# The last half chunk of a projection done as 64-row matmul pairs that open their sums, four output tiles at a time

## The chip, the cores and the metric

One core of a Trainium2 chip runs the kernel. The metric is the device time of one execution in microseconds (us). Times of runs below are medians of six executions, those of the kernel before medians of eleven (six in the first comparison). The kernel before takes 150.12 us (three executions, 150.08 to 150.18). The profile's span is shorter than that by about 1.7 us, because it runs from the first to the last recorded instruction.

TensorE is called PE below, its weight loads PEld, VectorE DVE, ScalarE ACT, GpSimd POOL and SyncE SP, as in the profile.

## The reference

Input x has 2048 tokens of 448 features. Two branches are mixed by a gate computed from each token:

```python
def reference(A_x, A_wqkv, A_w_phi, A_wo, B_x, B_w1, B_b1, B_w2, B_b2, gate_w):
    g = sigmoid((A_x * gate_w).sum(-1, keepdims=True))
    # A: linear attention, 16 heads of 28; phi is a pair of softmaxes of q @ w_phi and k @ w_phi
    o = num / den                      # phi_q @ (phi_k^T v)  over  phi_q @ sum(phi_k)
    a = o.reshape(S, 448) @ A_wo
    # B: dense 448 -> 1792 -> 448 with a tanh gelu
    b = gelu(B_x @ B_w1 + B_b1) @ B_w2 + B_b2
    return g * a + (1 - g) * b
```

In the kernel B's input is x too. The last stage works on 16 output tiles of 128 tokens. A tile's PSUM sum `y` collects 14 matmuls of the dense product (1792 = 14 x 128) and the attention product, whose contraction is 448 = 3.5 x 128: three full chunks and half a chunk.

## The kernel before

The output stage of the kernel before, with cuts marked. `oT` holds the attention result transposed; `oT[:, 3]` has 64 rows of it, then a row of ones that multiplies b2 (stored as row 64 of `wo_sb[:, 3]`), then zeros.

```python
    def num_tile(t):                                    # numerators of tile t
        nm = ps2.tile([P, 512], F32, name="nm", tag="nm", bufs=2)       # two PSUM banks
        for x in range(NPR):                            # 8 matmuls of 58 columns
            nc.tensor.matmul(nm[...], lhsT=EqT[:, x, tok], rhs=KV[:, x, :], start=True, stop=True)
        ...                                             # VectorE: den, reciprocal, al
        nc.vector.tensor_tensor(out=o_tok[:, t % 4, 0:D]..., in0=nmv..., in1=al..., op=ALU.mult)
        nc.sync.dma_start_transpose(oT[:, :, tok], o_tok[:, t % 4, :])

    def dense_out(y, t, cols):
        for j in range(NJ):                             # 14 matmuls
            nc.tensor.matmul(y, lhsT=gel[...], rhs=w2_sb[:, j, cols], start=(j == 0), stop=False)

    def attn_out(y, t, cols):
        for c in range(NC4):                            # 4 matmuls, the last with 64 useful rows + b2
            nc.tensor.matmul(y, lhsT=oT[:, c, tok], rhs=wo_sb[:, c, cols],
                             start=False, stop=(c == NC4 - 1))
        res = work.tile([P, D], BF16, name="res", bufs=3)
        nc.scalar.activation(out=res[:, cols], in_=y, func=ACT.Copy, scale=ungate[:, t:t + 1])
        nc.sync.dma_start(out2[tok, cols], res[:, cols])
    ...
    for t in range(NT - 1):
        dense_out(y[:, 0:D], t, full)
        ...                          # numerators of t + 2 (up to 8), later of t + 3: one tile a turn
        while len(wait) > (1 if t < 4 else 0):
            attn_out(*wait.pop(0))
    ...                              # tile 15 in two column parts, 336 and 112
```

`y` has four PSUM banks, `nm` two. Earlier in the kernel the input projections already use 64-row pairs: two matmuls with 64 contraction rows each, one on the upper and one on the lower half of the array, run at the same time.

The softmax here doesn't subtract the row's maximum and nothing guards it: scores larger than these inputs give would overflow.

Of the kernel before, what the change touches and what calls it, by code (L numbers as in the profile page):

```python
# [7 lines left out]
ALU = mybir.AluOpType  # L8
ACT = mybir.ActivationFunctionType
# [4 lines left out]
D = 448  # L14
# [3 lines left out]
P = 128  # L18
NB = 4
NT = 16  # L20
NG = 4
GW = 112
NC4 = 4
NJ = 14
KW = 60
NPR = 8
PW = 56
NK = 7
HP = 64

BF16 = mybir.dt.bfloat16
F32 = mybir.dt.float32
# [3 lines left out]
def kernel(  # L36
# [14 lines left out]
    nc = tc.nc  # L51
# [4 lines left out]
    consts = ctx.enter_context(tc.tile_pool(name="consts", bufs=1))  # L56
    work = ctx.enter_context(tc.tile_pool(name="work", bufs=2))
# [6 lines left out]
    def wide(name):  # L64
        return ps.tile([P, 2, 512], F32, name=name, tag="acc", bufs=1)
# [11 lines left out]
    w2_sb = consts.tile([P, NJ, D], BF16, name="w2_sb")  # L77
    wo_sb = consts.tile([P, NC4, D], BF16, name="wo_sb")
    EqT = consts.tile([P, NPR, S], BF16, name="EqT")
    phq3 = consts.tile([P, 2, NPR, 2, HP], BF16, name="phq3")  # L80
    oT = consts.tile([P, NC4, S], BF16, name="oT")
    o_tok = consts.tile([P, 4, 512], BF16, name="o_tok")
    KV = consts.tile([P, NPR, PW + 2], BF16, name="KV")
    mask = consts.tile([P, PW + 2], BF16, name="mask")
# [5 lines left out]
    ungate = consts.tile([P, NT], F32, name="ungate")  # L90

    hold = ctx.enter_context(tc.tile_pool(name="hold", bufs=1))
    phik = hold.tile([P, NT, NPR, 2, HP], BF16, name="phik", tag="phik_gel")
    vaug = hold.tile([P, NT, NPR, PW + 2], BF16, name="vaug")

    atn = ExitStack()
    attn = atn.enter_context(tc.tile_pool(name="attn", bufs=1))
# [14 lines left out]
    def q_tok(u):  # L112
        if u == 7:
            return phq3[:]
        return phq[u // 4][:, u % 4].rearrange("p (i x s w) -> p i x s w", i=2, x=NPR, s=2)
# [31 lines left out]
    def swap_x(h, part=None):  # L147
# [4 lines left out]
        if part != "even":  # L152
# [29 lines left out]
                          in_=mask[:, PW:PW + 2, None].to_broadcast([P, 2, DH]))  # L182
# [56 lines left out]
    def k_both(base, xo, b1=False):  # L239
        pks = both("pk", Wpk, WkS, D, base, xo, b1)  # L240
        for m, pk in enumerate(pks):
            k_exp(base // 2 + m, pk)
        if b1:
            nc.scalar.copy(out=b1T[:], in_=pks[1][:, 1, 480:480 + NJ])
# [43 lines left out]
    def norm(dst, split):  # L288
        sums = work.tile([P, 32, 2], F32, name="sums", bufs=3)
        ph = dst.rearrange("p t x s w -> p (t x s) w")[:, :, 0:PW]  # L290
        ph = ph.rearrange("p y (h d) -> p y h d", d=DH)
        nc.vector.reduce_sum(out=sums[:], in_=ph, axis=AX.X)  # L292
        rec = work.tile([P, 32, 2], F32, name="rec", bufs=3)
        nc.vector.reciprocal(out=rec[:], in_=sums[:])  # L294
        parts = [(nc.vector, 0, split), (nc.gpsimd, split, 32)] if split else [(nc.gpsimd, 0, 32)]
        for eng, lo, hi in parts:
            eng.tensor_tensor(out=ph[:, lo:hi], in0=ph[:, lo:hi],  # L297
                              in1=rec[:, lo:hi, :, None].to_broadcast([P, hi - lo, 2, DH]),
                              op=ALU.mult)
# [4 lines left out]
    def q_norm(u):  # L304
        norm(q_tok(u), 0)
        for i in range(2):
            t = 8 * (u // 4) + 4 * i + u % 4
            nc.sync.dma_start_transpose(EqT[:, :, t * P:(t + 1) * P],
                                        q_tok(u)[:, i].rearrange("p x s w -> p (x s w)"))
# [45 lines left out]
    def kv_sum(acc, u):  # L355
        for t in (2 * u, 2 * u + 1):
            for x in range(NPR):
                nc.tensor.matmul(acc[:, 0, x * (PW + 2):(x + 1) * (PW + 2)],  # L358
                                 lhsT=phik[:, t, x, :, :].rearrange("p s w -> p (s w)"),
                                 rhs=vaug[:, t, x, :], start=(t == 0 and x == 0),  # L360
                                 stop=(t == NT - 1), skip_group_check=True)

    def kv_out(acc):
        nc.vector.tensor_tensor(
            out=KV[:], in0=acc[:, 0, 0:NPR * (PW + 2)].rearrange("p (x w) -> p x w", x=NPR),
            in1=mask[:, None, :].to_broadcast([P, NPR, PW + 2]), op=ALU.mult)
# [61 lines left out]
    nc.sync.dma_start(wo_sb[:, 0:3, :], A_wo[0:384, :].rearrange("(c p) n -> p c n", p=P))  # L428
    nc.sync.dma_start(wo_sb[0:64, 3, :], A_wo[384:448, :])
    nc.sync.dma_start(wo_sb[64:65, 3, :], B_b2[None, :])  # L430

    k_both(0, x0o)
    k_norm(0)
# [29 lines left out]
    def m_unit(h, j):  # L463
        hp = wide("hp") if h == 0 and j == 2 else pair("hp")
        for k in range(NK):
            for i in range(2):
                nc.tensor.matmul(hp[:, i, :],  # L467
                                 lhsT=w1_sb[i * HP:(i + 1) * HP, k, j * P:(j + 1) * P],
                                 rhs=x_half(i, k, h), start=(k == 0), stop=(k == NK - 1))
        if gel[h] is None:  # L470
            gel[h] = hold.tile([P, NJ, S // 2], BF16, name="gel1", tag="phik_gel")
        nc.scalar.activation(out=gel[h][:, j, :],  # L472
                             in_=hp[:].rearrange("p a b -> p (a b)"),
                             func=ACT.Gelu_apprx_tanh, bias=b1T[:, j:j + 1])

    def num_tile(t):
        tok = slice(t * P, (t + 1) * P)
        nm = ps2.tile([P, 512], F32, name="nm", tag="nm", bufs=2)
        for x in range(NPR):
            nc.tensor.matmul(nm[:, x * (PW + 2):(x + 1) * (PW + 2)], lhsT=EqT[:, x, tok],  # L480
                             rhs=KV[:, x, :], start=True, stop=True)
        nmv = nm[:, 0:NPR * (PW + 2)].rearrange("p (x w) -> p x w", x=NPR)
        den = work.tile([P, NPR, 2], F32, name="den", bufs=3)
        nc.vector.tensor_scalar(out=den[:], in0=nmv[:, :, PW:PW + 2], scalar1=1e-6, scalar2=None,  # L484
                                op0=ALU.add)
        nc.vector.reciprocal(out=den[:], in_=den[:])
        al = work.tile([P, NPR, 2], F32, name="al", bufs=3)
        nc.vector.tensor_scalar(out=al[:], in0=den[:], scalar1=eL[:, t:t + 1], scalar2=None,
                                op0=ALU.mult)
        nc.vector.tensor_tensor(  # L490
            out=o_tok[:, t % 4, 0:D].rearrange("p (x h d) -> p x h d", x=NPR, h=2),
            in0=nmv[:, :, 0:PW].rearrange("p x (h d) -> p x h d", h=2),
            in1=al[:, :, :, None].to_broadcast([P, NPR, 2, DH]), op=ALU.mult)
        nc.sync.dma_start_transpose(oT[:, :, tok], o_tok[:, t % 4, :])

    for n in range(2 * NJ):
        m_unit(n // NJ, n % NJ)
        if n < 8:
            q_norm((0, 1, 2, 3, 4, 5, 6, 7)[n])
        if n == 8:  # L500
            nc.sync.dma_start(w2_sb[:], B_w2.rearrange("(j p) n -> p j n", p=P))
        if n == 4:
            acc = wide("acc")
            for u in range(8):
                kv_sum(acc, u)
            kv_out(acc)
            gates()

    psx.close()
    ps2 = ctx.enter_context(tc.tile_pool(name="ps2", bufs=2, space=PSUM, reuse_waits="tile"))  # L510


    def dense_out(y, t, cols):
        for j in range(NJ):
            nc.tensor.matmul(y, lhsT=gel[t // 8][:, j, (t % 8) * P:(t % 8 + 1) * P],  # L515
                             rhs=w2_sb[:, j, cols], start=(j == 0), stop=False)

    def attn_out(y, t, cols):
        tok = slice(t * P, (t + 1) * P)
        for c in range(NC4):  # L520
            nc.tensor.matmul(y, lhsT=oT[:, c, tok], rhs=wo_sb[:, c, cols],  # L521
                             start=False, stop=(c == NC4 - 1))
        res = work.tile([P, D], BF16, name="res", bufs=3)
        nc.scalar.activation(out=res[:, cols], in_=y, func=ACT.Copy, scale=ungate[:, t:t + 1])  # L524
        nc.sync.dma_start(out2[tok, cols], res[:, cols])

    def y_tile():
        return ps2.tile([P, 512], F32, name="y", tag="y", bufs=4)

    y = y_tile()  # L530
    num_tile(0)
    num_tile(1)
    wait = []
    full = slice(0, D)
    for t in range(NT - 1):
        y = y_tile() if t else y
        dense_out(y[:, 0:D], t, full)
        wait.append((y[:, 0:D], t, full))
        for n in ([t + 2] if t < 6 else [8, 9] if t == 6 else [t + 3]):
            if n < NT:  # L540
                num_tile(n)
        while len(wait) > (1 if t < 4 else 0):
            attn_out(*wait.pop(0))
    for cols in (slice(0, 336), slice(336, D)):
        y = y_tile()[:, 0:cols.stop - cols.start]
        dense_out(y, NT - 1, cols)
        attn_out(y, NT - 1, cols)
# [1 line left out]
_INS = ['A_x', 'A_wqkv', 'A_w_phi', 'A_wo', 'B_x', 'B_w1', 'B_b1', 'B_w2', 'B_b2', 'gate_w']  # L549
_OUTS = [((1, 2048, 448), 'bfloat16')]  # L550
# [25 lines left out]
```

## Time and profile before

| what | value | where from |
|---|---|---|
| time | 150.12 us | median of 3 |
| span of the profile | 148.4 us | page |
| PE busy | 144.2 us, 97% | page, part 1 |
| output stage | 58.12 us | trace: start of the first numerator matmul (86.95) to start of the last matmul (145.08) |
| tail | 3.31 us | trace: start of the last matmul to the end of the span |

Starts are what to read on PE: a matmul's record is longer than the time for which it keeps the next one waiting (0.35 against 0.189 us at 448 columns). "Output stage" in this document always means the stretch defined in the table.

Two of the costliest groups of the page (line, engine, operation, shapes and count, then busy us and mean ns, then idle time before them), and the line of the DMA issues for the transposes (count, median us to landing):

```profile
L524 ACT ACTIVATE res<-y,ungate 128x448 bf16<-128x448 f32 (+2 forms) x17 | 10.4, 613 | 47.1 <-PE y L521 41.1
...
L521 PE MATMUL y<-wo_sb,oT 128*128 128x448 bf16 (+2 forms) x68 | 14.7, 341 | 0.0
...
oT<-o_tok SPq DMA_TRANSPOSE x16, 2.4
```

ScalarE evicts the output and waits for PE; PE waits for nobody (0.0 idle). A transpose takes 2.4 us from issue to landing in the median (tile 9's took 4.0).

### The profile page before, as it was taken

The page shows a single profiled execution, that of the slowest core. Times are in us where ns is not written, and L with a number is a line of the kernel's source. Part 1 is how long each engine was busy: PE and PEld are TensorE (multiplying, and loading weights), DVE is VectorE, ACT ScalarE, POOL GpSimd, SP SyncE. Part 2 cuts the span into 40 slices and gives each one's busy share as a digit, 9 for nine tenths or more (in the row PEclk, how much of TensorE's full clock was granted, in tenths as well). Part 3 has the DMA queues.
Part 4 walks back from the last instruction along what each step waited for, and adds up shares of the span by engine and source line. Part 5 has one row for each costly group of instructions (what it writes and reads, how often), then busy time and mean ns, then how long its engine had stood idle before and what let it go on. Part 6 is the DMA issues. An engine that isn't in the chain of part 4 may idle for free.

```text
span 148.4 us, 3123 instructions
## 1 busy us (share of the span) xinstructions
PE 144.2 (97%) x1302; PEld 75.7 (51%) x1302; DVE 79.5 (54%) x129; ACT 75.6 (51%) x93; POOL 68.4 (46%) x50
## 2 busy tenths in 40 slices
PE   7999999999999999999999999999999999999991
PEld 2674445554544944444444455555555555555561
DVE  3443799999999999999100046333336333333000
ACT  1656989988899337676777760111311111111121
POOL 7999999999877999929930000000000000000000
PEclk9999999999999999999999999999999999999999
DMA  4999999999400199990999903333212422223201
GB/s 144 239 234 208 171 180 214 218 217 214 107 2 2 24 175 142 191 180 15 169 174 200 313 0 71 62 75 70 67 65 70 102 67 70 71 71 76 79 31 31
DMA packets 44658, 17.85 MB, mean 120 GB/s; under 512 B 36706, under 2 KB 44644, under 8 KB 44644
## 3 DMA queue, kind: packets, MB, share of 16 engines
q1 hardware_dynamic: 43428, 16.99, 55.0%
q10 hardware_dynamic: 1152, 0.65, 1.6%
q8 instruction: 10, 0.16, 0.5%
q14 instruction: 4, 0.03, 0.1%
q0 software_dynamic: 64, 0.01, 0.0%
HBM read 6.11 MB, written 1.84 MB: 54 GB/s over the span
## 4 chain that ended last, share of the span: by engine, by line
PE 97%; ACT 0%; issue 0%; DVE 0%; ACTq 0%
PE hp L467 29%; PE y L515 29%; PE y L521 8%; PE pq L351 7%; PE v_ps L335 4%; PE pk L343 4%; PE pk L226 3%; PE acc L358 3%; PE nm L480 3%; PE warm_ps L389 2%; PE v_ps L212 2%; PE v_ps L226 2%; PE w_ps L253 1%; PE xp L372 1%; PE pk L229 1%; PE v_ps L229 0%
## 5 line engine op out<-in xcount | busy, mean ns | idle before, releaser
L515 PE MATMUL y<-w_sb,gel 128*128 128x448 bf16 (+2 forms) x238 | 45.2, 341 | 0.0
L467 PE MATMUL hp<-xT,w_sb 64*128 64x512 bf16 x196 | 42.6, 376 | 0.0
L467 PE MATMUL hp<-xS,w_sb 64*128 64x512 bf16 x196 | 42.6, 376 | 0.0
L472 ACT ACTIVATE gel<-hp,b1T 128x1024 bf16<-128x1024 f32 x28 | 30.8, 1111 | 13.2 <-PE hp L467 13.2
L524 ACT ACTIVATE res<-y,ungate 128x448 bf16<-128x448 f32 (+2 forms) x17 | 10.4, 613 | 47.1 <-PE y L521 41.1
L515 PEld LDWEIGHTS <-gel 128*128 128x128 bf16 x238 | 22.6, 98 | 19.6
L467 PEld LDWEIGHTS <-w_sb 64*128 64x128 bf16 x392 | 18.9, 94 | 23.1
L297 POOL TENSOR_TENSOR phik<-phik,rec 128x1792 bf16<-128x1792 bf16 (+1 forms) x8 | 24.9, 3127 | 1.7 <-DVE rec L294 1.6
L484 DVE TENSOR_SCALAR den<-nm 128x16 f32<-128x16 f32 x16 | 2.8, 174 | 42.7 <-PE nm L480 42.7
L292 DVE TENSOR_REDUCE sums<-phik 128x64 f32<-128x1792 bf16 x8 | 16.0, 1999 | 3.5 <-ACT phik L283 3.5
L521 PE MATMUL y<-wo_sb,oT 128*128 128x448 bf16 (+2 forms) x68 | 14.7, 341 | 0.0
L297 POOL TENSOR_TENSOR oT<-oT,rec 128x1792 bf16<-128x1792 bf16 x4 | 12.7, 3209 | 1.1 <-DVE rec L294 1.1
L351 PE MATMUL pq<-Wpq,xT 64*128 64x448 bf16 x56 | 11.4, 349 | 0.0
L351 PE MATMUL pq<-WqS,xS 64*128 64x448 bf16 x56 | 11.4, 349 | 0.0
L297 POOL TENSOR_TENSOR w_sb<-w_sb,rec 128x1792 bf16<-128x1792 bf16 x3 | 9.6, 3210 | 2.9 <-DVE rec L294 2.9
L490 DVE TENSOR_TENSOR o_tok<-nm,al 128x448 bf16<-128x448 f32 x16 | 10.0, 625 | 0.6
L294 DVE RECIPROCAL rec<-sums 128x64 f32<-128x64 f32 x16 | 8.9, 553 | 1.4
L200 DVE CAST vaug<-v_ps 128x896 bf16<-128x896 f32 x7 | 7.5, 1072 | 2.4 <-PE v_ps L212 2.1
L282 ACT ACTIVATE phik<-pk 128x896 bf16<-128x896 f32 x8 | 7.6, 953 | 1.5 <-PE pk L231 1.5
L292 DVE TENSOR_REDUCE sums<-oT 128x64 f32<-128x1792 bf16 x4 | 7.9, 1981 | 0.0
L283 ACT ACTIVATE phik<-pk 128x896 bf16<-128x896 f32 x8 | 7.7, 964 | 0.0
L521 PEld LDWEIGHTS <-oT 128*128 128x128 bf16 x68 | 5.6, 97 | 3.5
(111 smaller groups left out, 170.5 us busy)
## 6 DMA issues: line engine op xcount, KB each, us to landing
w_sb<-in_B_w_dram SPq DMA_DIRECT2D x4, 784.0 KB, 11.8
out_dram<-res SPq DMA_DIRECT2D x15, 112.0 KB, 1.9
w_sb<-in_B_w_dram SPq DMA_DIRECT2D x1, 1568.0 KB, 7.2
xS<-xT SPq DMA_DIRECT2D x2, 256.0 KB, 3.7
EqT<-in_A_x_dram ACTq DMA_DIRECT2D x1, 448.0 KB, 3.3
xS<-xT SPq DMA_DIRECT2D x2, 192.0 KB, 3.5
wo_sb<-in_A_wo_dram SPq DMA_DIRECT2D x1, 336.0 KB, 16.8
oT<-o_tok SPq DMA_TRANSPOSE x16, 2.4
```

Source lines behind the costliest of these rows:

```text
L282: nc.scalar.activation(out=dst[:, :, :, 0, 0:PW], in_=src, func=ACT.Exp)
L283: nc.scalar.activation(out=dst[:, :, :, 1, 0:PW], in_=src, func=ACT.Exp, scale=-1.0)
L292: nc.vector.reduce_sum(out=sums[:], in_=ph, axis=AX.X)
L294: nc.vector.reciprocal(out=rec[:], in_=sums[:])
L297: eng.tensor_tensor(out=ph[:, lo:hi], in0=ph[:, lo:hi], in1=rec[:, lo:hi, :, None].to_broadcast([P, hi - lo, 2, DH]), op=ALU.mult)
L351: nc.tensor.matmul(pq[:, i, 0:D], lhsT=x_half(i, k, h)[:, r * P:(r + 1) * P], rhs=w_half(Wpq, WqS, i, k), start=(k == 0), stop=(k == NK - 1))
L467: nc.tensor.matmul(hp[:, i, :], lhsT=w1_sb[i * HP:(i + 1) * HP, k, j * P:(j + 1) * P], rhs=x_half(i, k, h), start=(k == 0), stop=(k == NK ...
L472: nc.scalar.activation(out=gel[h][:, j, :], in_=hp[:].rearrange("p a b -> p (a b)"), func=ACT.Gelu_apprx_tanh, bias=b1T[:, j:j + 1])
L490: nc.vector.tensor_tensor(out=o_tok[:, t % 4, 0:D].rearrange("p (x h d) -> p x h d", x=NPR, h=2), in0=nmv[:, :, 0:PW].rearrange("p x (h d) ...
L515: nc.tensor.matmul(y, lhsT=gel[t // 8][:, j, (t % 8) * P:(t % 8 + 1) * P], rhs=w2_sb[:, j, cols], start=(j == 0), stop=False)
L521: nc.tensor.matmul(y, lhsT=oT[:, c, tok], rhs=wo_sb[:, c, cols], start=False, stop=(c == NC4 - 1))
L524: nc.scalar.activation(out=res[:, cols], in_=y, func=ACT.Copy, scale=ungate[:, t:t + 1])
```

## The change

The intent: the half chunk of the attention product occupies PE as long as a full one. If two tiles' half chunks sit on different 64-row halves of the array, they can run as one pair in the time of one matmul. To have few switches between full-height and half-height matmuls, four tiles' half chunks come together, and they come first, so they *open* the four sums. Then b2 can't ride in row 64 any more; ScalarE makes a tile b2 x (1 - g), and VectorE evicts `y` with one multiply-add. Six banks let four sums be open while earlier ones are read.

The core of the diff (cuts marked with ...):

```diff
+    wo3 = consts.tile([P, D], BF16, name="wo3")          # the last 64 rows of wo, twice
...
+        if t % 2 and t > 3:                              # odd tiles: a copy for the lower half
+            nc.vector.tensor_copy(out=o_tok[:, t % 4, D:512], in_=o_tok[:, t % 4, D - HP:D])
...
+    def ends(ys, t):
+        for i in range(2):
+            for y, cols in ys[i]:
+                nc.tensor.matmul(y, lhsT=oT[i * HP:(i + 1) * HP, 3, (t + i) * P:(t + i + 1) * P],
+                                 rhs=wo3[i * HP:(i + 1) * HP, cols], start=True, stop=False)
...
+        else:
+            nc.vector.scalar_tensor_tensor(out=res[:, cols], in0=y, scalar=ungate[:, t:t + 1],
+                                           in1=b2u[t][:, cols], op0=ALU.mult, op1=ALU.add)
...
-        return ps2.tile([P, 512], F32, name="y", tag="y", bufs=4)
+        return ps2.tile([P, 512], F32, name="y", tag="y", bufs=6)
...
+    for t in range(4):                                   # tiles 0-3 as before, 4 chunks
+        dense_out(y[:, 0:D], t, full, True, (6, 7) if t == 2 else ())   # 6, 7 after 7 of 14 matmuls
+        for n in ([2, 3], [4, 5], [], [])[t]:
+            num_tile(n)
...
+    for g in range(4, NT, 4):
...
+        ends(group[0:2], g)
+        ends(group[2:4], g + 2)
+        for t in range(g, g + 4):
+            b2_tile(t)
+            for y, cols in group[t - g]:
+                dense_out(y, t, cols, False)
+                if t - g < 2 and g + 4 < NT:
+                    for n in (2 * t - g + 4, 2 * t - g + 5):
+                        num_tile(n)
+                attn_out(y, t, cols, 3)
```

More of the change, by code (lines that the diff above doesn't have):

```diff
@@ L93 @@
     phik = hold.tile([P, NT, NPR, 2, HP], BF16, name="phik", tag="phik_gel")
-    vaug = hold.tile([P, NT, NPR, PW + 2], BF16, name="vaug")
+    vaug = hold.tile([P, NT, NPR, PW + 2], BF16, name="vaug", tag="vaug_b2")
     atn = ExitStack()
@@ L430 @@
     nc.sync.dma_start(wo_sb[64:65, 3, :], B_b2[None, :])
+    for i in range(2):
+        nc.sync.dma_start(wo3[i * HP:(i + 1) * HP, :], A_wo[384:448, :])
     k_both(0, x0o)
@@ L499 @@
             q_norm((0, 1, 2, 3, 4, 5, 6, 7)[n])
+        if n == 5:
+            b2_sb = hold.tile([P, D], BF16, name="b2_sb", tag="vaug_b2")
+            nc.sync.dma_start(b2_sb[:], B_b2[None, :].to_broadcast([P, D]))
         if n == 8:
@@ L510, with dense_out, attn_out, b2_tile @@
     ps2 = ctx.enter_context(tc.tile_pool(name="ps2", bufs=2, space=PSUM, reuse_waits="tile"))
-    def dense_out(y, t, cols):
+    def dense_out(y, t, cols, opens, mid=()):
         for j in range(NJ):
+            if j == NJ // 2:
+                for n in mid:
+                    num_tile(n)
             nc.tensor.matmul(y, lhsT=gel[t // 8][:, j, (t % 8) * P:(t % 8 + 1) * P],
-                             rhs=w2_sb[:, j, cols], start=(j == 0), stop=False)
-    def attn_out(y, t, cols):
+                             rhs=w2_sb[:, j, cols], start=(opens and j == 0), stop=False)
+    def ends(ys, t):
+        for i in range(2):
+            for y, cols in ys[i]:
+                nc.tensor.matmul(y, lhsT=oT[i * HP:(i + 1) * HP, 3, (t + i) * P:(t + i + 1) * P],
+                                 rhs=wo3[i * HP:(i + 1) * HP, cols], start=True, stop=False)
+    def attn_out(y, t, cols, chunks):
         tok = slice(t * P, (t + 1) * P)
-        for c in range(NC4):
+        for c in range(chunks):
             nc.tensor.matmul(y, lhsT=oT[:, c, tok], rhs=wo_sb[:, c, cols],
-                             start=False, stop=(c == NC4 - 1))
+                             start=False, stop=(c == chunks - 1))
         res = work.tile([P, D], BF16, name="res", bufs=3)
-        nc.scalar.activation(out=res[:, cols], in_=y, func=ACT.Copy, scale=ungate[:, t:t + 1])
+        if chunks == NC4:
+            nc.scalar.activation(out=res[:, cols], in_=y, func=ACT.Copy, scale=ungate[:, t:t + 1])
+        else:
+            nc.vector.scalar_tensor_tensor(out=res[:, cols], in0=y, scalar=ungate[:, t:t + 1],
+                                           in1=b2u[t][:, cols], op0=ALU.mult, op1=ALU.add)
         nc.sync.dma_start(out2[tok, cols], res[:, cols])
+    b2u = {}
+    def b2_tile(t):
+        b2u[t] = work.tile([P, D], F32, name="b2u", bufs=2)
+        nc.scalar.activation(out=b2u[t][:], in_=b2_sb[:], func=ACT.Copy, scale=ungate[:, t:t + 1])
     def y_tile():
-        return ps2.tile([P, 512], F32, name="y", tag="y", bufs=4)
+        return ps2.tile([P, 512], F32, name="y", tag="y", bufs=6)
+    full = slice(0, D)
+    parts = [slice(0, 336), slice(336, D)]
     y = y_tile()
@@ L533 @@
     wait = []
-    full = slice(0, D)
-    for t in range(NT - 1):
+    for t in range(4):
         y = y_tile() if t else y
-        dense_out(y[:, 0:D], t, full)
-        wait.append((y[:, 0:D], t, full))
-        for n in ([t + 2] if t < 6 else [8, 9] if t == 6 else [t + 3]):
-            if n < NT:
-                num_tile(n)
-        while len(wait) > (1 if t < 4 else 0):
-            attn_out(*wait.pop(0))
-    for cols in (slice(0, 336), slice(336, D)):
-        y = y_tile()[:, 0:cols.stop - cols.start]
-        dense_out(y, NT - 1, cols)
-        attn_out(y, NT - 1, cols)
+        dense_out(y[:, 0:D], t, full, True, (6, 7) if t == 2 else ())
+        wait.append((y[:, 0:D], t, full, NC4))
+        for n in ([2, 3], [4, 5], [], [])[t]:
+            num_tile(n)
+        while len(wait) > (1 if t < 3 else 0):
+            attn_out(*wait.pop(0))
+    for g in range(4, NT, 4):
+        group = []
+        for t in range(g, g + 4):
+            group.append([(y_tile()[:, 0:c.stop - c.start], c)
+                          for c in (parts if t == NT - 1 else [full])])
+        ends(group[0:2], g)
+        ends(group[2:4], g + 2)
+        for t in range(g, g + 4):
+            b2_tile(t)
[3 more added lines that the diff above has]
+                    for n in (2 * t - g + 4, 2 * t - g + 5):
+                        num_tile(n)
+                attn_out(y, t, cols, 3)
 _INS = ['A_x', 'A_wqkv', 'A_w_phi', 'A_wo', 'B_x', 'B_w1', 'B_b1', 'B_w2', 'B_b2', 'gate_w']
```

## The prediction

> **What bounds the kernel now.** I read the page first (busy time, slices, chain), then the timeline of TensorE and VectorE over the last 60 us, then the view of waits.
>
> ```profile
> PE 144.2 (97%) x1302; PEld 75.7 (51%) x1302; DVE 79.5 (54%) x129; ACT 75.6 (51%) x93; POOL 68.4 (46%) x50
> ...
> PE   7999999999999999999999999999999999999991
> ...
> PEclk9999999999999999999999999999999999999999
> ...
> PE 97%; ACT 0%; issue 0%; DVE 0%; ACTq 0%
> ```
>
> TensorE (PE) is the chain: 97% of it, at full granted clock, in every slice. A change counts only if it shortens PE's instruction stream, makes PE wait, or alters the tail of some 3 us after its last matmul. The attention product is line 521 (68 matmuls), the dense product line 515, the numerator tiles line 480. In the output stage (from 86.95 us) PE's timeline has no gap:
>
> ```profile
> 100.43 0.92 PE L521 MATMUL y<-wo_sb,oT 128*128 128x448 bf16 x4
> 101.19 2.81 PE L515 MATMUL y<-w_sb,gel 128*128 128x448 bf16 x14
> 103.83 0.39 PE L480 MATMUL nm<-KV,EqT 128*128 128x58 bf16 x8
> 104.06 1.67 PE L521 MATMUL y<-wo_sb,oT 128*128 128x448 bf16 x8
> ```
>
> From the starts, 14 matmuls of 448 columns take 103.83 - 101.19 = 2.64 us, so one takes 0.189 us of PE (the 0.35 us in the groups is its latency, which overlaps), and a numerator tile (8 matmuls) 104.06 - 103.83 = 0.23 us. VectorE works in bursts:
>
> ```profile
> 87.39 0.17 DVE L484 TENSOR_SCALAR den<-nm 128x16 f32<-128x16 f32 x1 [16.46 <-PE nm L480]
> ...
> 88.16 0.62 DVE L490 TENSOR_TENSOR o_tok<-nm,al 128x448 bf16<-128x448 f32 x1
> 88.70 0.17 DVE L484 TENSOR_SCALAR den<-nm 128x16 f32<-128x16 f32 x1
> ...
> 89.45 0.63 DVE L490 TENSOR_TENSOR o_tok<-nm,al 128x448 bf16<-128x448 f32 x1
> 90.49 0.17 DVE L484 TENSOR_SCALAR den<-nm 128x16 f32<-128x16 f32 x1 [0.41 <-PE nm L480]
> ```
>
> Two numerator tiles back to back are taken up every 88.70 - 87.39 = 1.31 us, and the first gives its PSUM bank back 88.16 + 0.62 - 87.39 = 1.39 us after it was begun. Tile 2's numerators start at 90.06 in PE's timeline and VectorE begins at 90.49: 0.43 us later.
>
> The kernel already contains what the change adds, 64-row pairs between full-height matmuls:
>
> ```profile
> 10.94 2.43 PE L226 MATMUL pk<-Wpk,xT 128*128 128x448 bf16 x12
> 13.30 0.36 PE L229 MATMUL pk<-WkS,EqT 64*128 64x448 bf16 x1
> 13.31 0.36 PE L231 MATMUL pk<-Wpk,xT 64*128 64x448 bf16 x1
> 13.50 0.35 PE L229 MATMUL pk<-WkS,EqT 64*128 64x448 bf16 x1
> 13.51 0.35 PE L231 MATMUL pk<-Wpk,xT 64*128 64x448 bf16 x1
> 13.79 0.18 PE L220 MATMUL pk<-ident,w_sb 128*128 128x14 bf16 x1
> ```
>
> The two of a pair start together. The last full-height matmul starts at 10.94 + 11 x 0.189 = 13.02; the next full-height one at 13.79. Take off that first one's own 0.19 and two pairs cost 0.58 us. Bare they would cost 2 x 0.189 = 0.38, so entering and leaving the pairs costs 0.20, some 0.1 us each way.
>
> **What the Trainium skill says.** "TensorEngine Tiling (Array Packing)", section Key Properties: different tiles of the array run in parallel, and "Changing tiling mode (not just tile) drains the TensorE". The trace agrees with both: 0.01 us between the two starts, and the 0.1 us at each switch. "TensorE: Matmul & The Clock Gate", section Back-to-back issue gap, gives N / 2.4 + 2.5 ns for an isolated gap, 189 ns at N = 448, which is what the trace has (the same section gives lower figures for streams; this trace doesn't show them). "VectorE: DVE Perf Modes", section Why PSUM operands drop a tier: an fp32 PSUM operand leaves VectorE at one element a cycle; at the page's 0.96 GHz 448 elements are 0.47 us, and the trace has 0.625 us for the 128x448 product out of PSUM, so I take 0.625 for the new VectorE eviction of the same size.
>
> **The change part by part.**
>
> (a) *Pairs.* In tiles 4 to 15 the fourth chunk leaves the full-height stream. For four tiles it costs 4 x 0.189 = 0.757 us now; as two pairs it costs 0.58 by the pattern above. Gain 0.177 us a group, 0.53 us for three groups. In the last group tile 15's half chunk is a 336 and a 112 column matmul on one half of the array; together they are 448 columns beside tile 14's, so the same sum.
>
> (b) *Numerators in twos.* Still 16 tiles; 0.45 us a pair against twice 0.23: no gain from the grouping itself. But there are two numerator banks, so a tile's numerators cannot start before VectorE has read the tile two before. In the changed kernel the pairs come as (0,1), (2,3) after dense 0, (4,5) after dense 1, (6,7) in the middle of dense 2. From the measured durations:
> - 2 starts at 90.06, 3 at 90.29. Tile 1 was released at 89.45 + 0.63 = 90.08: just free.
> - 4 starts at 90.52 + 2.65 = 93.17, 5 at 93.40. VectorE begins 2 at 90.49, 3 at 91.80, and releases 3 at 93.19: just free.
> - attention 0 runs 93.63 to 94.38, seven dense matmuls to 95.71: 6 starts there, 7 is due at 95.94. VectorE begins 4 at 93.60, 5 at 94.91, and releases 5 at 96.30. With the hand-over and the weight load that waits with it (a LDWEIGHTS record is 0.1 us), I take 0.45 us of PE standing still.
> The later pairs come 3.67 us apart (0.46 + three chunks 0.57 + dense 2.65) while VectorE needs 2 x 1.31, a small copy and one eviction, 3.5 to 3.6 in all: no wait, and the group after has three full tiles of slack.
>
> (c) *VectorE eviction, ScalarE bias tile.* Twelve of each per run, on engines with idle time in this stage (ScalarE has 41.1 us of waiting for PE ahead of its evictions): off PE's path. Six output banks let a group of four open while the former one's last tiles are still being read, so I expect no bank wait.
>
> (d) *Transposes.* Opening the sums needs all four oT tiles of the group early. Tile 7: numerators end near 96.6, VectorE ends near 99.3 with the extra copy, landing 2.4 us later (DMA issues, median) at 101.7. PE reaches the pairs at 96.6 + 1.32 + 0.76 + 2.65 + 1.51 = 102.8. Hidden, with 1.1 us to spare. In later groups the margin is over 1.5 us.
>
> (e) *Tail.* The last eviction (112 columns) is 0.36 us on ScalarE, beginning 0.09 after the matmul record ends. VectorE's would be about 0.28 (estimate: 0.625 less 336 elements at 0.96 a ns) and begins 0.04 after. Gain about 0.1 us.
>
> (f) *Loads.* The extra wo and b2 loads come on a queue that PE doesn't wait for here: nothing.
>
> Sum: -0.53 + 0.45 - 0.1 = -0.18 us: 150.12 becomes **149.95 us**.
>
> **The rivals.**
> - *No wait at numerator 7* (VectorE is quicker, or PE slower, than I reckon): only the gains stay, 149.5 us. Against it: the six durations it is made of are steady in the trace (all evictions of the numerators 0.62 to 0.63 us).
> - *Free switches*: were two pairs to cost 0.38, the gain would be 3 x 0.38 = 1.14 and the time 149.3 with the wait, 148.9 without. Against it: the 0.58 at 13.0 us, and the same again at 15.9 us.
> - *A transpose late*: some landings take up to 4 us rather than 2.4 (the tile view's longest). One such for tile 7 outlasts the margin by 0.5 us, a second wait: 150.4 to 150.5.
> - *VectorE becomes the bound in the groups*: four numerator tiles and four evictions per group are 4 x 1.31 + 4 x 0.63 + copies = 8 us in some 14 us of PE. Not likely.
>
> **Range and chances.** Of the terms, the wait (0 to 0.55) and a late transpose (0 to 0.5) are the uncertain ones; the pair saving is read from the same pattern. Low end: no wait and a somewhat larger saving, 149.4. High end: both waits, 150.5. All of these are within 0.6 us, and 2% would be 3.0 us: faster by over 2% 0.01, within 2% 0.98, slower 0.01.
>
> **What would show it.** Right: each group of four half-height matmuls takes 0.58 us from full-height start to full-height start (less one matmul); the waits show PE or its weight load waiting for VectorE about 0.4 us ahead of one numerator tile, that of tile 7, near 96 us, with no other PE gap of over 0.1 us after 87 us; PE's last matmul starts some 0.1 us earlier than now; the last VectorE eviction is near 0.28 us. Wrong: PE waiting for a DMA ahead of the pairs (transpose late), pairs at 0.38 or above 0.75, a wait ahead of every later numerator pair, or PE waiting on an output bank.

## The result, and the profile after

The changed kernel takes 150.24 us (150.10 to 150.58, six executions) against 150.11 us for the kernel before in the same rounds. Ratios here are the mean time of one kernel's fast runs over that of the other's fast runs of the same rounds, so not quite the ratio of the medians: 1.0008, with a 95% interval of 0.9995 to 1.0022. That is "the same". In us the interval runs from -0.08 to +0.33.

Busy time and chain on the page of the changed kernel:

```profile
PE 143.3 (97%) x1302; PEld 74.2 (50%) x1302; DVE 88.1 (59%) x148; ACT 75.5 (51%) x92; POOL 68.4 (46%) x50
...
PE 89%; DMA 3%; SPq 2%; DVE 2%; issue 0%
```

PE has lost 0.9 us of busy time, and yet the span is 148.4 us as before. The chain is no longer PE alone: DVE and DMA stand in it. What the page's chain gives to DMA lies mostly at the head (it names the WqT load); the 2% of DVE lie in the output stage, and the view of waits has the line that the kernel before does not have:

```profile
PE nm L483 <- DVE o_tok L493: 0.3, 1, 0.3
```

One wait, of PE for VectorE's product that reads a numerator bank. The timeline of PE shows where (start, length, engine, line, operation, count; in brackets the idle time before it and its releaser):

```profile
94.49 1.49 PE L526 MATMUL y<-w_sb,gel 128*128 128x448 bf16 x7
95.82 0.39 PE L483 MATMUL nm<-KV,EqT 128*128 128x58 bf16 x8
96.55 0.39 PE L483 MATMUL nm<-KV,EqT 128*128 128x58 bf16 x8 [0.34 <-DVE o_tok L493]
96.78 1.49 PE L526 MATMUL y<-w_sb,gel 128*128 128x448 bf16 x7
...
101.50 1.68 PE L538 MATMUL y<-wo_sb,oT 128*128 128x448 bf16 x8
103.11 0.55 PE L532 MATMUL y<-wo,oT 64*128 64x448 bf16 x4
103.60 2.82 PE L526 MATMUL y<-w_sb,gel 128*128 128x448 bf16 x14
```

Tile 6's eight numerators start at 95.82, tile 7's should start 0.23 later at 96.05 and start at 96.55: 0.50 us lost from start to start (the 0.34 in brackets is counted from the end of the last record). And the gain: the eighth attention matmul starts at 101.50 + 7 x 0.189 = 102.82, the next full-height one at 103.60; less that eighth's own 0.19, two pairs cost 0.59 us with both switches. Four full-height matmuls would cost 0.757.

VectorE's timeline at the same place, to be set against the one shown of the kernel before in the prediction:

```profile
95.02 0.17 DVE L487 TENSOR_SCALAR den<-nm 128x16 f32<-128x16 f32 x1
...
95.78 0.62 DVE L493 TENSOR_TENSOR o_tok<-nm,al 128x448 bf16<-128x448 f32 x1
96.44 0.18 DVE L498 COPY o_tok<-o_tok 128x64 bf16<-128x64 bf16 x1
```

This is tile 5: its bank is free when the product ends, at 95.78 + 0.62 = 96.40, and PE goes on 0.15 us later. The busy time of PE over the whole output stage is 57.78 of 58.12 us; before it was all of 58.13.

### The profile page after: what moved, and what is told of

It reads as the page before. It is cut to its first block, busy times and chain, and to the rows that moved or that the text cites. A ratio compares the mean times of both kernels' runs of the same rounds, so it can differ in the third digit from the quotient of the medians.

```text
span 148.4 us, 3147 instructions
## 1 busy us (share of the span) xinstructions
PE 143.3 (97%) x1302; PEld 74.2 (50%) x1302; DVE 88.1 (59%) x148; ACT 75.5 (51%) x92; POOL 68.4 (46%) x50
## 4 chain that ended last, share of the span: by engine, by line
PE 89%; DMA 3%; SPq 2%; DVE 2%; issue 0%
PE hp L470 29%; PE y L526 28%; PE pq L352 7%; PE y L538 6%; PE v_ps L336 4%; PE pk L344 4%; DMA WqT<-in_A_wqkv_dram 3%; PE pk L227 3%; PE acc L359 3%; PE nm L483 2%; SPq L146 2%; PE v_ps L227 2%; PE y L532 1%; DVE o_tok L493 1%; PE w_ps L254 1%; PE pk L230 1%
## 5 line engine op out<-in xcount | busy, mean ns | idle before, releaser
L552 ACT ACTIVATE b2u<-b_sb,ungate 128x448 f32<-128x448 bf16 x12 | 7.9, 666 | 28.7 <-DVE res L544 28.7
L544 DVE SCALAR_TENSOR_TENSOR res<-y,ungate,b2u 128x448 bf16<-128x448 f32 (+2 forms) x13 | 8.4, 648 | 16.3 <-PE y L538 16.3
L538 PE MATMUL y<-wo_sb,oT 128*128 128x448 bf16 (+2 forms) x55 | 12.4, 342 | 0.0
L542 ACT ACTIVATE res<-y,ungate 128x448 bf16<-128x448 f32 x4 | 2.5, 633 | 13.1 <-PE y L538 13.1
L283 ACT ACTIVATE phik<-pk 128x896 bf16<-128x896 f32 x8 | 7.6, 956 | 2.0 <-PE pk L232 2.0
```

The source lines that it names most:

```text
L283: nc.scalar.activation(out=dst[:, :, :, 0, 0:PW], in_=src, func=ACT.Exp)
L544: nc.vector.scalar_tensor_tensor(out=res[:, cols], in0=y, scalar=ungate[:, t:t + 1], in1=b2u[t][:, cols], op0=ALU.mult, op1=ALU.add)
L552: nc.scalar.activation(out=b2u[t][:], in_=b2_sb[:], func=ACT.Copy, scale=ungate[:, t:t + 1])
```

## The experiments

Each run was timed in five rounds beside the kernel before on the same chip. The times of one kernel spread over 0.3 to 1.5 us between executions, mostly 0.3 to 0.8, which is as much as most of the effects here or more; by the 2% measure every run below is "the same". So the output stage of each run's profile is given beside its median; it repeats to 0.01 us where nothing waits for a DMA. The waits in the table are worked out from the starts in the traces: the gap less what the same two matmuls take where nothing waits.

| run | stage starts | output stage | waits of PE in it | median | before |
|---|---|---|---|---|---|
| before, first profile | 86.95 | 58.12 | none | 150.12 | |
| changed, first profile | 87.07 | 58.12 | 0.50 bank | 150.24 | 150.11 |
| a0_after (changed) | 87.43 | 58.33 | 0.50 bank, 0.21 transpose | 150.59 | 150.32 |
| e1_seven_later | 86.91 | 57.89 | 0.26 transpose | 150.15 | 150.32 |
| e2_no_pairs | 87.21 | 58.62 | 0.50 bank | 150.89 | 150.32 |
| e3_pair_by_pair | 86.94 | 58.75 | 0.50 bank | 150.97 | 150.32 |
| b1_before | 86.85 | 58.12 | none | 150.07 | 150.36 |
| b2_loads | 86.91 | 58.13 | none | 150.11 | 150.36 |
| e4_out_on_act | 87.03 | 58.37 | 0.74 transpose | 149.89 | 150.36 |
| e5_pair_two_three | 86.95 | 58.04 | 0.60 transpose | 149.49 | 150.36 |
| b3_before | 87.33 | 58.12 | none | 150.16 | 150.11 |
| a3_after (changed) | 87.01 | 58.12 | 0.50 bank | 150.28 | 150.11 |
| e6_earlier_numerators | 87.09 | 57.44 | none | 149.37 | 150.11 |
| e7_stores_on_sync | 87.25 | 57.48 | none over 0.05 | 149.75 | 150.11 |

### a0_after: the changed kernel again (no edit)

> The changed kernel once more, as the reference for the runs beside it. Output stage (start of the first numerator matmul to start of the last matmul) 58.12 us as in its first profile, with one TensorE gap of 0.50 us ahead of tile 7's numerators. Time: if the 0.12 us later start of the output stage in its first profile was chance, the median is within 0.1 us of the kernel before; if the extra loads cause it, the output stage begins 0.1 us or more later than in the kernel before (86.95) again, and the median is 0.1 us or more above it.

The gap of 0.50 us ahead of tile 7's numerators is there again, and the stage starts at 87.43. Both marks that the expectation set for the extra loads are met: the late start, and a median 0.27 us above the kernel before. b2_loads below has these loads alone and shows neither; the kernel before itself started at 87.33 once (b3_before). And the stage is 0.21 us longer than in the first profile. A second wait, in the second group's pairs, does it (timeline of PEld):

```profile
118.23 0.09 PEld L532 LDWEIGHTS <-oT 64*128 64x128 bf16 x1 [0.29 <-DMA oT<-o_tok]
```

The weight load of the group's fourth half chunk, tile 11, waits for that tile's transpose. The expectation did not foresee it.

a3_after is the changed kernel once more. It was run at another time. Expected beforehand: a stage of 58.1 to 58.4 us and a time 0 to 0.3 us above the null run beside it (b3_before). It had 58.12 us and 0.12 us (150.28 against 150.16).

### e1_seven_later: tile 7's numerators half a tile later

```diff
-        dense_out(y[:, 0:D], t, full, True, (6, 7) if t == 2 else ())
+        dense_out(y[:, 0:D], t, full, True, (6,) if t == 2 else ())
-        for n in ([2, 3], [4, 5], [], [])[t]:
+        for n in ([2, 3], [4, 5], [7], [])[t]:
```

> Tile 7's numerators after dense 2 rather than right behind tile 6's. Theory (the wait for tile 5's read of the bank eats the pairs' gain): the gap goes, nothing else moves, output stage 57.62 us (58.12 - 0.50), time 0.5 us below the changed kernel of this call, about 149.7. Rival (the gain was lost elsewhere, or the wait only moves to the pairs, because tile 7's transpose is late): output stage 58.0 or more, a gap ahead of the first half-height matmul.

The bank wait is gone: tile 7's numerators now follow the dense matmuls without a gap. But of the 0.50 us only 0.23 comes out (58.12 to 57.89), because PE now arrives at the pairs earlier, and there it stands for tile 7's transpose (PE and PEld):

```profile
102.45 0.82 PE L532 MATMUL y<-wo,oT 64*128 64x448 bf16 x4
...
102.91 0.09 PEld L532 LDWEIGHTS <-oT 64*128 64x128 bf16 x1 [0.35 <-DMA oT<-o_tok]
```

So both were partly right: the bank wait is real and removable, and behind it the rival of the late transpose holds half of the gain. Without that 0.26 us wait the stage would be 57.63, as the theory had it. Against the changed kernel of the same call the median is 0.44 us lower (150.15 to 150.59), and the stages differ by 0.44 too.

Why the transpose is late is told by SyncE's timeline in the changed kernel:

```profile
97.94 1.44 SPq L546 DMA_DIRECT2D out_dram<-res  x1
99.46 2.51 SPq L499 DMA_TRANSPOSE oT<-o_tok  x2
```

The store of tile 0 occupies the queue for 1.44 us ahead of the transposes of tiles 6 and 7, and each of these two takes 1.19 us to issue. Tile 7's copy on VectorE ends at 99.43, but its transpose is issued at 100.78 and, at 2.3 us to landing (the tile view of these two), is there at 103.1. The pairs begin at 103.11, tile 7's own at 103.31. The spare time was at most 0.2 us, not the 1.1 us of the prediction (0.6 us in a0_after, where tile 7 landed at 103.06 and its matmul started at 103.67).

In e1's own profile the delay is shared out differently:

```profile
97.77 0.53 SPq L546 DMA_DIRECT2D out_dram<-res  x1
98.39 3.35 SPq L499 DMA_TRANSPOSE oT<-o_tok  x2
```

Here the store takes 0.53 us and tile 6's transpose 2.02 us to issue, and tile 7's is again issued 1.28 us after its copy ended (100.54 against 99.26). So the store ahead is not all of it: in every profile with the new order one issue at about 98 us is stretched, either that store (1.4 to 1.5 us in place of 0.5) or tile 6's transpose (1.7 to 2.0 us in place of 1.2). In the three profiles of the kernel before it is tile 4's transpose, with 1.9 to 2.5 us. No run shows why.

### e2_no_pairs: the half chunks at full height

```diff
-                nc.tensor.matmul(y, lhsT=oT[i * HP:(i + 1) * HP, 3, ...],
-                                 rhs=wo3[i * HP:(i + 1) * HP, cols], start=True, stop=False)
+                nc.tensor.matmul(y, lhsT=oT[:, 3, ...], rhs=wo3[:, cols], start=True, stop=False)
+    nc.vector.memset(wo3[HP:P, :], 0.0)          # the lower half multiplies by zero
...                                             # wo3 is loaded into its upper half only
```

> The changed kernel with the half chunk done full-height (zeros in the lower half of its weights), same place and order, VectorE eviction and six banks kept. Theory (two pairs cost 0.58 us with their two switches, four full-height ones 0.757): output stage longer by 3 x 0.176 = 0.53, 58.65 us; time about 0.5 us above the changed kernel. Rival (switches are free, 0.38 per two pairs): longer by 3 x 0.38 = 1.14, 59.26 us. Rival (pairs gain nothing when they open their sums): 58.1 us.

Stage 58.62: 0.50 us longer than the changed kernel's 58.12, so the pairs gain 0.17 us a group. Predicted was 0.177. PE's timeline at the first group:

```profile
101.64 1.68 PE L538 MATMUL y<-wo_sb,oT 128*128 128x448 bf16 x8
103.15 0.92 PE L532 MATMUL y<-wo,oT 128*128 128x448 bf16 x4
103.91 2.43 PE L526 MATMUL y<-w_sb,gel 128*128 128x448 bf16 x12
```

Four full-height half chunks: 103.91 - 103.15 = 0.76 us and no gap at either end. Everything else of the change, VectorE's eviction, the six banks, the order, is in this run, so the 0.50 us is the pairs alone. The time is 0.30 us above a0_after's, whose stage had the extra 0.21 us.

### e3_pair_by_pair: six places instead of three

```diff
-        ends(group[0:2], g)
-        ends(group[2:4], g + 2)
         for t in range(g, g + 4):
+            if (t - g) % 2 == 0:
+                ends(group[t - g:t - g + 2], t)
```

> The changed kernel with each pair of tiles opened right before its own two tiles: six places with one pair in place of three with two, the same matmuls. Theory (each place costs two switches of 0.095): three places more, 3 x 0.19 = 0.57 us, output stage 58.69 us. Rival (no cost of a switch by itself): 58.12 us.

Stage 58.75, which is 0.63 us longer than the changed kernel's: 0.21 us for each of the three places added, a little over the 0.19 expected. The first group, PE:

```profile
102.98 0.36 PE L532 MATMUL y<-wo,oT 64*128 64x448 bf16 x2
103.27 2.82 PE L526 MATMUL y<-w_sb,gel 128*128 128x448 bf16 x14
```

From the start of the pair to the next full-height matmul 0.29 us, where the pair alone would take 0.19. At one pair per place the switches eat all of the gain: six places save 6 x 0.189 us and pay 6 x 0.2 us, and the stage is even 0.14 us longer than with no pairs at all (58.75 against e2's 58.62). This also rules out that switches are free.

### b1_before and b3_before: the kernel before as a run (no edit)

> The kernel before, unchanged, as a run of its own: a second profile of it and a null measurement. Expected ratio 1.000 within its interval. If the start of the output stage (86.95 us in its first profile, 86.91 to 87.43 in five profiles of changed kernels) varies from execution to execution, it will not be 86.95 again by more than 0.1 us; if it is a property of the kernel before, it will be within 0.05 of 86.95. Output stage 58.12 us, no TensorE gap.

> The kernel before once more, as the null beside the next three: ratio 1.000, or 0.999 as its first run of this kind (0.9986); output stage 58.12 us, starting at 86.85 to 87.0.

Their ratios to the kernel before are 0.9986 (0.9968 to 1.0004) and 0.9997 (0.9975 to 1.0020). A difference of 0.2 us in a time is therefore not resolved by one such run. The stage is 58.124 us in all three profiles of the kernel before. Its start is not a constant: 86.95, 86.85 and 87.33. The later start in the first profile of the changed kernel (87.07) is within that spread; a0_after's 87.43 lies 0.1 us above it.

### b2_loads: only the three extra loads and their tiles

```diff
+    wo3 = consts.tile([P, D], BF16, name="wo3")
+    for i in range(2):
+        nc.sync.dma_start(wo3[i * HP:(i + 1) * HP, :], A_wo[384:448, :])
+        if n == 5:
+            b2_sb = hold.tile([P, D], BF16, name="b2_sb", tag="vaug_b2")
+            nc.sync.dma_start(b2_sb[:], B_b2[None, :].to_broadcast([P, D]))
```

> The kernel before plus the three extra loads and their tiles alone (nothing uses them). Theory (the later start in the profiles of the changed kernel is chance): ratio to the kernel before 1.000 within 0.1%, output stage 58.12 us. Rival (the loads or the moved addresses delay the head): the output stage begins 0.1 to 0.4 us later than in the kernel before, time 0.1 to 0.4 us more.

Start 86.91, stage 58.13, ratio 0.9989 (0.9969 to 1.001): the loads cost nothing that these runs can see.

### e4_out_on_act: e1 with the stores on ScalarE's queue

```diff
-        nc.sync.dma_start(out2[tok, cols], res[:, cols])
+        (nc.sync if t > 12 else nc.scalar).dma_start(out2[tok, cols], res[:, cols])
```

> Tile 7's numerators later, as before, and the output stores of tiles 0 to 12 issued from ScalarE's queue in place of SyncE's, so that the transposes stand alone there. Theory (the transposes of tiles 7 and 11 come late to the pairs because they queue behind one another and the stores on SyncE): tile 7's transpose issues right when VectorE is done (near 99.4) and lands by 101.9, no wait ahead of the pairs, output stage 57.62 us, time 0.5 us below the kernel before. Rival (landings are slow whatever queue the stores use): waits of 0.2 to 0.3 us ahead of a pair stay, stage 57.8 to 57.9.

Half a miss. The first group's wait is gone, as expected: its two pairs and switches take 0.48 us from first start to next full-height start. Tile 7's transpose is issued at 99.68, which is 0.98 us earlier than in e1, both counted from the start of the stage. But the second group now waits for tile 11's transpose for 0.74 us:

```profile
117.87 0.36 PE L532 MATMUL y<-wo,oT 64*128 64x448 bf16 x1 [0.39 <-DMA oT<-o_tok]
```

That transpose was issued at 112.75 and took 5.1 us to land, in place of 2.3. In the three profiles of the changed kernel the same transpose took 4.2, 4.5 and 4.0 us, with the stores on SyncE. So stores on SyncE are not needed for the second group's wait; the rival was right there. (With the stores on ScalarE it took 5.1 us here and 4.9 in e5, with the stores on SyncE 3.8 to 4.5 in six profiles.)

What these profiles have in common at that place is a 16 KB transfer of the queue that the page calls "instruction" (at 114.5, 115.8 and 114.3 us in the changed kernel, 115.0 here), and packets of the transposes or of a store that take 1.4 to 2.4 us each where 0.02 to 0.04 us are usual. The traces of all runs show more of this. In the 14 profiles 32 of the 202 transposes of the output stage with a recorded landing took over 3 us, and during every one of the 32 such a 16 KB transfer was under way. The kernel before has them too, where nobody waits: tile 9's took 4.0, 4.3 and 3.9 us, with no packet over 0.13 us at that place. But 13 other transposes had a transfer and took 2.3 to 2.9 us. The two coincide; no run here tells which holds up which, or whether a third thing holds up both. Less its wait the stage is 57.63 again.

### e5_pair_two_three: one more pair at the same switches

```diff
+        if g == 4:                                       # tiles 2, 3: close as a pair
+            b2_tile(2); b2_tile(3)
+            ends([[(y, full)] for y in y23[2:4]], 2, False)       # start=False, stop=True
         ends(group[0:2], g)
         ends(group[2:4], g + 2)
+        if g == 4:
+            for t in (2, 3):
+                out_tile(y23[t], t, full, 3)             # evicted by VectorE with b2
```

> The former kernel with one more pair: tiles 2 and 3 close their sums as a 64-row pair right ahead of the first group's two pairs, so at the same two switches. Theory (a pair that shares its switches gains a whole matmul): output stage shorter by 2 x 0.189 - 0.197 = 0.18 us than in the former kernel, 57.44 us; time 0.2 us less. Rival (the saving per pair is 0.09, half of what two pairs gain): 0.09 us less.

The stage has a transpose wait of 0.60 us in the second group; without it, it is 57.44, against 57.63 without waits in e1 and e4. A pair that shares its switches gains the whole of a matmul, 0.19 us. The measured time is 149.49 us, ratio 0.9941 (0.9922 to 0.9961). That is 0.40 us below e4's median where 0.2 was expected, and the intervals of the two ratios overlap (e4: 0.9955 to 0.9996).

### e6_earlier_numerators: the second and third groups' transposes get one tile more time

```diff
-        for n in ([2, 3], [4, 5], [7], [])[t]:
+        for n in ([2, 3], [4, 5], [7], [8, 9])[t]:
-                if t - g < 2 and g + 4 < NT:
-                    for n in (2 * t - g + 4, 2 * t - g + 5):
-                        num_tile(n)
+                for n in {4: [10, 11], 7: [12, 13], 8: [14, 15]}.get(t, []):
+                    num_tile(n)
```

> The kernel with the pair of tiles 2 and 3, and the numerators of tiles 8 to 15 issued one tile earlier, so that their transposes have 3.2 us more. Theory (the waits of 0.41 and 0.55 us ahead of the second group's pairs are late transposes): no wait ahead of any pair of tiles 8 to 15, output stage 57.44 us (58.12 - 0.53 - 0.18 + a few hundredths), time 0.6 to 0.7 us below the null run. Rival (the wait moves to VectorE's banks or to the output banks): a gap of 0.2 us or more ahead of a numerator or a pair.

Stage 57.435 us, as worked out beforehand, and no wait of PE anywhere in it. Three pairs at the first group, PE:

```profile
102.72 0.74 PE L532 MATMUL y<-wo,oT 64*128 64x448 bf16 x6
103.39 0.93 PE L526 MATMUL y<-w_sb,gel 128*128 128x448 bf16 x4
```

0.67 us for three pairs and the way back, one pair (0.19) more than the 0.48 of two. The time is 149.37 us (148.97 to 149.54), 0.79 below the null run; the ratio to the kernel before is 0.9943 (0.9917 to 0.9968). It is below both kernels, by about half a per cent. Two things to note: the waits of e5 and e4 are 0.60 and 0.74 us from start to start, so the 0.41 and 0.55 of the expectation are short by one matmul each; and this run's ratio is no better than e5's 0.9941, so that the earlier numerators save time over e5 is shown by the stage of one profile each, not by the times.

### e7_stores_on_sync: the same with all stores on SyncE

```diff
-        (nc.sync if t > 12 else nc.scalar).dma_start(out2[tok, cols], res[:, cols])
+        nc.sync.dma_start(out2[tok, cols], res[:, cols])
```

> The same with all stores back on SyncE's queue. If the queue for the stores matters, tile 7's transpose is late again by 0.2 to 0.3 us ahead of the first group's pairs (output stage 57.65 to 57.75); if it was only the order of events, 57.44 as with the stores on ScalarE.

Stage 57.48: 0.05 us more than e6, at the first group's pairs. The expected 0.2 to 0.3 us did not come. The queue still sets when tile 7's transpose lands: 16.00 us after the start of the stage here, 15.96 in e1, and 15.15 in e6 with the stores on ScalarE. But in this order PE asks for it 0.27 us later than in e1: 0.19 for the pair of tiles 2 and 3, which goes first, and 0.08 because two matmuls left the stretch ahead and two numerator tiles came into it. So of e1's wait of 0.26 us only 0.04 is left. The medians (149.75 and 149.37) differ by more, and the intervals of the two ratios (0.9948 to 1.0001 and 0.9917 to 0.9968) overlap, so a difference is not shown.

## Why the prediction was right or wrong

The forecast was 149.95 us, in a range of 149.4 to 150.5, "within 2%" at 0.98. The measured 150.24 us lies in the range and the class is right. The sign is not: a gain of 0.18 us was forecast and none appeared; the forecast ratio would be 149.95 / 150.12 = 0.9989, just outside the measured interval (0.9995 to 1.0022). The null runs show how little such a distance means: an unchanged kernel read 0.9986 once.

Going through its steps:

- **(a) Pairs.** Right: forecast 0.53 us, measured 0.50 (e2). The pattern at 13 us in the kernel before gave the cost of the new places, including the switches.
- **(b) The bank wait.** Right, and the reason that the change gains nothing. Forecast: 0.45 us ahead of tile 7's numerators, due to VectorE's reading of tile 5. Measured: 0.50 at that place, with that releaser, in every profile that has this order; e1 takes it away. The term was short by 0.05 us. Pairs and wait together leave the stage at 58.116 against 58.124.
- **(c) Eviction and six banks.** Right that they are off PE's path: no profile has PE waiting for an output bank. The forecast duration of 0.625 us was too small; the groups by form show VectorE's multiply-add at 0.684 and ScalarE's bias tile at 0.666:

```profile
L552 ACT ACTIVATE b2u<-b_sb,ungate 128x448 f32<-128x448 bf16 x12 | 7.9, 666 | 28.7 <-DVE res L544 28.7
L544 DVE SCALAR_TENSOR_TENSOR res<-y,ungate,b2u 128x448 bf16<-128x448 f32 x11 | 7.5, 684 | 14.3 <-PE y L538 14.3
```

- **(d) Transposes.** This is the step that failed: "Hidden, with 1.1 us to spare. In later groups the margin is over 1.5 us." It put the transpose at VectorE's end plus 2.4 us and left out the queue: the store of tile 0 and the issue of tile 6's transpose held tile 7's back by 1.35 us. Without stores on that queue it was issued 0.98 us earlier (e4); the rest goes with the stretched issue at about 98 us, whose cause stays open. In the first group the margin was 0.2 us or less in two of three profiles, and that tile 7 was in time there was luck: the bank wait had already delayed PE. In the second group, where the margin was to be over 1.5 us, tile 11's transpose takes 4.0 to 4.5 us to land, and one of the three profiles of the changed kernel waits 0.21 us for it; why it lands so late stays open too (see e4). The rival "a transpose late" was named for tile 7; what it was worth in the changed kernel is 0 to 0.2 us by execution, at tile 11, and as much again became visible as soon as the bank wait was taken away.
- **(e) Tail.** Mis-sized. The last eviction, before on ScalarE (first fence) and after on VectorE (second):

```profile
145.38 0.36 ACT L524 ACTIVATE res<-y,ungate 128x112 bf16<-128x112 f32 x1 [0.34 <-PE y L521]
```

```profile
145.44 0.33 DVE L544 SCALAR_TENSOR_TENSOR res<-y,ungate,b2u 128x112 bf16<-128x112 f32 x1 [0.21 <-PE y L538]
```

  It is 0.33 us, not 0.28; with the earlier begin the gain is some 0.07 us at most. And the tail after it is made of store landings: it is 3.26, 3.33 and 3.49 us in the three profiles of the changed kernel, 3.31, 3.30 and 3.30 in those of the kernel before, and 3.11 in b2_loads and 3.03 to 3.05 in e5 to e7, for no reason that a run shows. No gain of 0.1 us can be read from these.
- **(f) Loads.** Right, by b2_loads.
- **The rivals.** "No wait at numerator 7" and "free switches" are ruled out by the profile after and by e3. "VectorE becomes the bound in the groups": no later numerator waits for it.

The sum with measured sizes is -0.50 + 0.50, a transpose wait of 0 to 0.2, and a tail between -0.05 and +0.18: between nothing and some 0.4 us slower, which is in line with what the runs of the changed kernel show (0.13, 0.27 and 0.17 us above the kernel before of the same call, in medians). Whether it is truly slower or the same isn't settled by them: one of the three intervals of the changed kernel (a0_after's, 1.0002 to 1.0038) excludes equality, and the other two don't.

## What to carry to other kernels

A saving on the engine that bounds the kernel is collected only if nothing that feeds it is asked for earlier than before: this change saved 0.50 us of matmuls, the new order of the numerators took 0.50 us back, and the early demand for the transposes took 0 to 0.21 us more. Before trusting a margin on a DMA, add up its queue, with what is issued ahead of it and how long each issue takes, not only its own landing time. Half-height pairs paid here by the number of pairs per switch: one pair per place gained nothing, two gained 0.17 us, and a third at the same place gained a whole matmul (0.19 us).

## What the Trainium skill lacked or had wrong

- "TensorEngine Tiling (Array Packing)", section Key Properties, says that changing the tiling mode drains the engine and gives no cost. Measured here: 0.095 us on entering and 0.093 us on leaving 64-row mode after two pairs between streams of 448 columns (starts in the traces; 0.103 us on leaving after a single pair), and 0.21 us for each added place with one pair (e3).
- "TensorE: Matmul & The Clock Gate", section Back-to-back issue gap, gives about 131 ns per matmul of 512 columns for streams with weight loads in between. No stream here comes near: 512 columns take 216 ns (line 467 of the kernel before, 64-row pairs) and 448 columns 189 ns from start to start, with a weight load for each, which is the formula N / 2.4 + 2.5 that the same section keeps for isolated gaps.
- "Runtime: NRT & Kernel Launch", section Instruction fetch mechanics, calls the cost of crossing a 16 KiB instruction block "mostly hidden". In the 14 profiles here a 16 KB transfer of the instruction queue was under way during every one of the 32 output-stage transposes that took over 3 us to land, in place of 2.3 to 2.4, and in three profiles PE waits for such a one (0.21 us in a0_after, 0.74 in e4, 0.60 in e5). The runs don't show that the one causes the other.
- No page has a duration for VectorE's scalar_tensor_tensor with an fp32 PSUM operand, an fp32 SBUF operand and a pointer scalar: 684 ns for 128x448 and 334 ns for 128x112, against 625 ns for the 128x448 tensor_tensor out of PSUM.
